# Identity products in TensorE's waits, two more units of cache kept in SBUF, and the first keys of the second layer in three pieces

## The chip, the cores and the metric

One core of one Trainium2 chip. The metric is the device time of the launch in microseconds, the median of several runs; lower is better.

## The reference

Two layers, each of which is an attention over a cached key and value store for one new token, and then a gated feed-forward block; both layers use the same weights and the same cache. Everything is 32-bit float.

```python
B, Sq, D = 2, 1, 512;  Hq, Hkv, Sk, Dh = 32, 8, 32768, 128;  Df = 1792
def _A_ref(x, k_cache, v_cache, wq, wo):
    q = (x @ wq)                       # per head, 4 query heads share one key head
    scores = einsum("bhqd,bhkd->bhqk", q, k) * (Dh ** -0.5)
    o = einsum("bhqk,bhkd->bhqd", softmax(scores), v)
    return o @ wo
def _B_ref(x, w_gate, w_up, w_down):
    return einsum("bsf,fd->bsd", gelu(x @ w_gate) * (x @ w_up), w_down)
x = A_x
x = x + _A_ref(_layernorm(x), ...);  x = x + _B_ref(_layernorm(x), ...)
x = x + _A_ref(_layernorm(x), ...);  x = x + _B_ref(_layernorm(x), ...)
```

The cache is the bulk: for each of 2 x 8 pairs of a sequence and a key head, 32768 keys and as many values of 128 numbers, 16 MB each.

## The kernel before

**Memory and units.** SBUF holds one large tile `M` of 110 units; a unit is 512 columns on 128 partitions, 256 KB. Units 0 to 95 are three slots of 32 (`SLOT_A`, `SLOT_B`, `SLOT_C`), each of which takes half of the keys or half of the values of one pair. Units 96 to 107 serve for weights; `PL` gives four places of 4 units there. `U_P0`, `U_P1`, `U_PT` (106 to 109) hold intermediate results when no weights stand there.

**The queue.** All loads are planned in one list in the order of their use, and SP issues them in this order. `free()` marks a unit as no longer needed; `pump()` then issues the loads at the head of the list whose places are free. An issue waits, on SP, for the instructions that read its place last, and for the landing of the load eight before it; all that is behind it in the list waits too.

**Attention.** `order1` gives the 16 pairs for the first layer; the second layer takes them in the opposite order, so that the last pair's cache can stay. For each pair, `scores` multiplies 32 key units per half (TensorE, `score_unit`, one unit is one product of 512 columns on one of four 32-row groups of the output bank), `peak` takes maxima, `softmax` exponentiates on ScalarE and transposes back, `values` multiplies 32 value units per half, and `combine` scales (ScalarE), transposes (TensorE) and reduces (VectorE). `project` adds the output projection into the bank `W`.

**Feed-forward.** `center` copies `W` (ScalarE), transposes it (TensorE) and makes the centred input (VectorE); `deviation` makes the norm's scale. `products(0)` and `products(1)` multiply 16 and 12 gate and up units, `gelu` is on ScalarE and VectorE, `hidden` transposes its result, and `down` multiplies 14 units. `restart` puts the residual back into `W`.

**The seam between the layers.** The last pair's values (64 units), the first 28 units of the second half of its keys (28 of `KC1`) and the last 5 units of the first half (in PSUM banks, `NPS`) are kept: 97 units. The other units of its keys are loaded again: 4 of the second half (`k1`) and 27 of the first half (`k0`, in pieces of 16 and 11, at units 64 to 90). In between the gate, up, down and query weights go through a ring of 16 units, in the order of `RING`: places 104, 92, 96 and 100, of 4 units each. The query products of the second layer alternate with scores on the kept keys. The keys of the second pair follow in pieces of 8, 8 and 16 at units 64 to 95, so that each needs the scores on the first pair's keys that stood there.

**The end.** The last layer's gate, up and down weights have slots of their own and no ring; they are loaded right behind the last values, and the last `down` is followed by one copy and the store.

PSUM banks in the order listings below: bank_79 is `A`, bank_80 is `W`, bank_81 is `X`, bank_74 and bank_75 take the scores.

Of the kernel before, what the change touches and what calls it, by code (L numbers as in the profile page):

```python
# [16 lines left out]
P = 128  # L17
# [18 lines left out]
PL = [96, 100, 104, 92]  # L36
# [10 lines left out]
KC1 = 28  # L47
NARROW = [6, 1]
NH = 2
NG = P // 16  # L50
WO_ORDER = {1: (2, 3, 0, 1)}
# [24 lines left out]
def block_kernel(ctx: ExitStack, tc: tile.TileContext, x, consts, kt, vt, wq, wo, wn, gu, wd, out):  # L76
# [90 lines left out]
    def ring_stream(name, l, src, total, at):  # L167
        cuts, places, n = [], [], 0
        while n < total:
            cuts.append(min(4, total - n))  # L170
            places.append(PL[RING[at % 4]])
            n += 4
            at += 1
        stream(name, l, src, total, cuts, places)
# [30 lines left out]
    for l in range(2):  # L205
        if l == 0:
            stream("wq", 0, wq, 32, (32,), (SLOT_C,))
            ring = [SLOT_A, SLOT_B, SLOT_C]
            todo = sequence(orders[0], 0)
            roles = [ring[(len(todo) - 4 + i) % 3] for i in range(3)]  # L210
        else:
            last0, last1, lastv = roles
            ring = [lastv, last0, last1]
            g, b = orders[1][0]
            assert last1 == SLOT_C
            add(("wq7",), cols(wq, 28, 4), ZONE + 2, 4)
            stream("wq", 1, wq, 28, (4, 2, 2, 4, 4, 4, 2, 2, 4), [ZONE + i for i in (6, 10, -4, -2, 2, 6, 10, -4, -2)])
            add(("k1",), cols(kt[b, g, 1], KC1, CH - KC1), ZONE + 2, CH - KC1)
            stream("k0", 1, kt[b, g, 0], KFREE, (16, 11), [last1, last1 + 16])
            g, b = orders[1][1]  # L220
            chunk("k", 1, g, b, 0, last1, (8, 8, 16))
            chunk("k", 1, g, b, 1, lastv)
            chunk("v", 1, g, b, 0, last0)
            add_wo(1, g)
            chunk("v", 1, g, b, 1, last1)
            todo = sequence(orders[1][2:], 1)
# [11 lines left out]
        if l == 0:  # L238
            ring_stream("gu", 0, gu, 28, 0)
            ring_stream("wd", 0, wd, 14, 7)  # L240
        else:
            stream("gu", 1, gu, 28, (8, 8, 4, 4, 4), [ring[(len(todo) - 3) % 3] + i for i in (0, 8, 16, 20, 24)])
            stream("wd", 1, wd, 14, (4, 4, 4, 1, 1), [ring[(len(todo) - 2) % 3] + i for i in (0, 4, 8, 12, 13)])
# [34 lines left out]
    def center():  # L278
        ws = mem(U_PT + 1)
        nc.scalar.activation(ws, W, AF.Copy, accum_out=rs)  # L280
        for c in range(KC):
            nc.tensor.transpose(X[:, c * P:(c + 1) * P], ws[:, c * P:(c + 1) * P], ident)
# [75 lines left out]
    def values(l, g, b, acc, wheres, keep, back):  # L358
        for h in range(2):
            where = wheres[h]  # L360
            for i in range(CH):
                key, u = where[i]
                if key:
# [4 lines left out]
                                 mem(u), start=(h == 0 and i < 4), stop=(h == 1 and i >= CH - 4))  # L368
                if not keep and i % back == back - 1:
# [3 lines left out]
    def combine(acc, oT, g, b):  # L373
        md = mem(U_PT)
        nc.scalar.activation(md, acc, AF.Copy, scale=linvc)  # L375
        for c in range(4):
# [29 lines left out]
    def feedforward(l):  # L406
# [8 lines left out]
        def products(v):  # L415
            s, nt = (0, 4) if v == 0 else (16, 3)
            for k in range(KC):
                for t in range(nt):
# [4 lines left out]
                    if cut[key] == s:  # L423
                        for q in range(28):
                            if where[q][0] == key:
                                free(where[q][1])
# [34 lines left out]
        def down(lo, hi):  # L461
            for n in range(lo, hi):
# [9 lines left out]
                free(un)  # L472

# [7 lines left out]
        hidden(1)  # L481
        down(8, FD)
# [10 lines left out]
    center()  # L493
# [15 lines left out]
    for n, (g, b) in enumerate(order1):  # L509
# [20 lines left out]
        values(0, g, b, A, [pieces[("v", 0, g, b, h)] for h in range(2)], (g, b) == last, CH)  # L530
        combine(A, oT, g, b)
# [17 lines left out]
    todo, s = deque(range(KC1)), 0  # L549
# [8 lines left out]
    for m in range(7):  # L558
# [10 lines left out]
        for j in range(min(early[m], len(todo))):  # L569
            i = todo.popleft()  # L570
            score_unit(S1, w, i, k1[i][1], i < 4, False)
# [4 lines left out]
    store(27, True)  # L576
    store(28, False)
# [7 lines left out]
    for i in range(KC1, CH):  # L585
        score_unit(S1, w, i, u + i - KC1, False, True)
    free(u, CH - KC1)
    peak(S1, 1)
# [18 lines left out]
    for n, (g, b) in enumerate(orders[1]):  # L607
# [7 lines left out]
        values(1, g, b, A, [pieces[("v", 1, g, b, h)] for h in range(2)], False, CH)  # L615
        combine(A, oT, g, b)
# [42 lines left out]
```

## Time and profile before

| | |
|---|---|
| runs | 2572.09, 2572.43, 2576.22 us |
| median | 2572.43 us |
| profiled execution, its own time | 2574.56 us |
| its span, first to last instruction | 2572.4 us |
| read from HBM | 1103.98 MB, 429 GB/s over the span |
| TensorE busy | 1354.3 us (53%) |
| mean granted TensorE clock | 0.741 |
| last values land, TensorE starts on them: first layer | 1285.50 us |
| the same, second layer | 2542.14 us |

A row of a timeline reads: start, length in us, engine, line, operation, output<-inputs, shape, number of instructions, and in brackets the idle time of the engine before it with what ended it. A 32-bit product stands in the trace as two records, a transpose as one. DMA issues stand with the engine that issues them (SPq), and a listing of issues ends with the time from issue to landing.

### The profile page before, as it was taken

To read this page: it belongs to the slowest core of one execution; us is meant where nothing else is said; L and a number is where in the kernel's file an instruction comes from. 1 tells how busy PE (TensorE), PEld (TensorE's weight loads), DVE (VectorE), ACT (ScalarE), POOL (GpSimd) and SP (SyncE) were. 2 spreads that over 40 slices of the span, in tenths; PEclk is the share of its full clock that TensorE was granted. 3 is DMA by queue.
4 is the path that set the end of the run, shared out by engine and by line. 5 is a ranking of instruction groups with operands and counts; after the bars stand their busy time and mean duration, and the time that the engine had idled before them with its cause. 6 is when DMAs were issued, how large, how long until landed. Compare 5 with 4: busy or idle time off the path is not lost.

```text
span 2572.4 us, 20214 instructions
## 1 busy us (share of the span) xinstructions
PE 1354.3 (53%) x9444; PEld 388.4 (15%) x9444; DVE 139.1 (5%) x459; ACT 83.4 (3%) x191; POOL 3.8 (0%) x12
## 2 busy tenths in 40 slices
PE   3545554445544555564576455454545544554556
PEld 1111111111111111111122111111111111111112
DVE  0000000000000000000011000000000000000001
ACT  0000000000000000000010000000000000000000
POOL 0000000000000000000000000000000000000000
PEclk9777777776777776777778777777777776777668
DMA  9999999999999999999999999999999999999998
GB/s 425 433 429 438 431 433 432 435 431 434 434 428 437 433 431 436 430 433 432 423 408 421 436 436 434 433 435 429 438 429 434 433 430 437 433 432 433 432 434 363
DMA packets 26187, 1105.34 MB, mean 430 GB/s; under 512 B 3032, under 2 KB 3288, under 8 KB 4312
## 3 DMA queue, kind: packets, MB, share of 16 engines
q1 hardware_dynamic: 25816, 1103.97, 99.5%
q8 instruction: 74, 1.21, 0.2%
q10 hardware_dynamic: 288, 0.09, 0.0%
q14 instruction: 9, 0.07, 0.0%
HBM read 1103.98 MB, written 0.07 MB: 429 GB/s over the span
## 4 chain that ended last, share of the span: by engine, by line
DMA 68%; PE 23%; another core or an unknown queue 8%; issue 0%; ACT 0%; DVE 0%; ACTq 0%; DVEq 0%; SPq 0%
DMA M<-in_vt 38%; DMA M<-in_kt 26%; PE bank L366 10%; PE bank L321 10%; DMA cst<-in_consts 2%; DMA M<-in_wd 1%; DMA M<-in_wq 1%; PE bank L297 1%; PE bank L421 0%; PE bank L388 0%; PE bank L377 0%; ACT M L375 0%; PE bank L402 0%; PE bank L349 0%
## 5 line engine op out<-in xcount | busy, mean ns | idle before, releaser
L321 PE MATMUL bank<-M,qw 128*32 128x512 f32 x4096 | 587.3, 736 | 534.7 <-DMA M<-in_kt 534.0
L366 PE MATMUL bank<-M 128*16 128x512 f32 x4096 | 578.3, 727 | 511.3 <-DMA M<-in_vt 511.3
L321 PEld LDWEIGHTS bank<-M,qw 128*32 128x32 f32 x4096 | 143.9, 132 | 966.7 <-DMA M<-in_kt 572.3
L366 PEld LDWEIGHTS bank<-M 128*16 128x16 f32 x4096 | 136.3, 112 | 926.5 <-issue 912.2
L324 DVE TENSOR_REDUCE sm<-bank 128x1 f32<-128x512 f32 x64 | 44.2, 691 | 1111.6 <-PE bank L321 1111.6
L346 ACT ACTIVATE M<-bank,sm 128x512 f32<-128x512 f32 x64 | 43.4, 682 | 1216.7 <-DVE sm L341 1216.7
L349 PE MATMUL bank<-cst,M 128*128 128x128 f32 x256 | 51.8, 353 | 42.2 <-ACT M L346 42.0
L380 DVE TENSOR_REDUCE oT<-bank 128x4 f32<-128x64 f32 x32 | 7.2, 224 | 1118.7 <-PE bank L377 1118.7
L375 ACT ACTIVATE M<-bank,sm 128x512 f32<-128x512 f32 x32 | 22.0, 687 | 1137.5 <-PE bank L366 1137.5
L350 DVE COPY M<-bank 128x512 f32<-128x512 f32 x64 | 43.9, 692 | 61.5 <-PE bank L349 61.5
L349 PEld LDWEIGHTS bank<-cst,M 128*128 128x128 f32 x256 | 37.8, 179 | 52.3 <-ACT M L346 52.3
L377 PE MATMUL bank<-cst,M 128*128 128x128 f32 x128 | 21.5, 291 | 25.8 <-ACT M L375 25.8
L340 PE MATMUL bank<-cst,sm 128*128 128x128 f32 x32 | 10.3, 323 | 35.1 <-DVE sm L339 35.1
L275 PE MATMUL bank<-cst,xin 128*2 128x128 f32 x32 | 5.0, 307 | 42.7 <-DMA cst<-in_consts 42.7
L421 PE MATMUL bank<-M,xw 128*32 128x512 f32 x112 | 21.0, 664 | 6.4 <-DMA M<-in_gu 4.3
L354 PEld LDWEIGHTS bank<-cst,sm 128*128 128x128 f32 x128 | 23.6, 258 | 0.0
L377 PEld LDWEIGHTS bank<-cst,M 128*128 128x128 f32 x128 | 13.7, 143 | 55.3 <-ACT M L375 55.3
L354 PE MATMUL bank<-cst,sm 128*128 128x4 f32 x128 | 21.4, 273 | 0.0
L297 PE MATMUL bank<-M,xw 128*32 128x512 f32 x128 | 19.7, 716 | 2.7 <-DMA M<-in_wq 1.9
L388 PE MATMUL bank<-M,oT 128*2 128x512 f32 x120 | 17.5, 621 | 5.1 <-DVE oT L380 5.1
L340 PEld LDWEIGHTS bank<-cst,sm 128*128 128x128 f32 x32 | 4.3, 133 | 64.1 <-DVE sm L339 64.1
L346 ACT ACTIVATION_READ_ACCUMULATOR M<-bank,sm 128x1 f32 x64 | 12.5, 196 | 0.0
(73 smaller groups left out, 140.4 us busy)
## 6 DMA issues: line engine op xcount, KB each, us to landing
M<-in_wo SPq DMA_DIRECT2D x6, 2048.0 KB, 53.1
M<-in_vt SPq DMA_DIRECT2D x6, 2048.0 KB, 43.9
M<-in_gu SPq DMA_DIRECT2D x10, 1024.0 KB, 17.0
M<-in_kt SPq DMA_DIRECT2D x2, 4096.0 KB, 15.1
M<-in_wd SPq DMA_DIRECT2D x6, 1024.0 KB, 16.5
M<-in_wq SPq DMA_DIRECT2D x6, 1024.0 KB, 8.7
M<-in_vt SPq DMA_DIRECT2D x4, 1024.0 KB, 47.1
M<-in_kt SPq DMA_DIRECT2D x2, 2048.0 KB, 11.0
```

What stands on the lines that cost most here:

```text
L297: nc.tensor.matmul(Q[32 * k:32 * k + 32, :], xw[:, k, XO - 2 * g:XO - 2 * g + 32], mem(u), start=start, stop=stop)
L321: nc.tensor.matmul(S[32 * t:32 * t + 32, :], w[:, 28 - 4 * c:60 - 4 * c], mem(u), start=start, stop=stop)
L324: nc.vector.tensor_reduce(mx[:, h:h + 1], S, axis=AX.X, op=OP.max)
L346: nc.scalar.activation(p[h], S[h], AF.Exp, bias=bias, scale=SCALE, accum_out=ls[:, h:h + 1])
L349: nc.tensor.transpose(S[h][:, k * P:(k + 1) * P], p[h][:, k * P:(k + 1) * P], ident)
L350: nc.vector.tensor_copy(mem(U_PT + h), S[h])
L354: nc.tensor.matmul(X[:, P:P + REP], ls[:, h:h + 1].to_broadcast([P, P]), mask, start=(h == 0), stop=(h == 1))
L366: nc.tensor.matmul(acc[32 * t:32 * t + 16, :], mem(U_PT + h)[:, k * P + 32 * t + 16 * e:k * P + 32 * t + 16 * e + 16], mem(u), start=(h == ...
L375: nc.scalar.activation(md, acc, AF.Copy, scale=linvc)
L377: nc.tensor.transpose(X[:, c * P:(c + 1) * P], md[:, c * P:(c + 1) * P], ident)
L388: nc.tensor.matmul(W[32 * t:32 * t + NB, :], oT[:, t, :], mem(u), start=(t > 0 and first), stop=final)
L421: nc.tensor.matmul(G[v][32 * t:32 * t + 32, :], xw[:, k, XO:XO + 32], mem(un), start=(k == 0), stop=(k == KC - 1))
```

## The change

Four things are changed together.

- **Kept and reloaded keys.** `KC1` goes from 28 to 30: 30 units of the second key half are kept (99 units in all), and 2 are loaded again. The ring loses two units: its places are 104 (4), 94 (2), 96 (4) and 100 (4), 14 units, and the weights' pieces are cut to fit. The order of the early scores, and the copies of the five units from PSUM to SBUF, are fitted to the new places.
- **The first half of these keys** comes in pieces of 8, 8 and 11 units in the place of 16 and 11.
- **Identity products.** `fill(n)` issues n products of 32 columns of the identity with the identity three times over (384 columns); the result goes to the last 32 partitions of `X`, columns 128 and up, and is read by nothing. They stand in the last `values` of each layer (3 after unit 15, 1 after unit 23, 3 after unit 27 of the second half), in the `combine` behind it (2), in each `center` but the first (2), after each piece of gate and up weights but the first and the last (half its units), after the fourth unit of `down` (2), and behind the second `hidden` (2): 54 in all, 27 from the first layer's last values to the first query products of the second layer, 27 from the second layer's last values on.
- **The last down weights** come in pieces of 4, 4, 2, 2, 1, 1 in the place of 4, 4, 4, 1, 1.

```diff
-PL = [96, 100, 104, 92]
+PL = [96, 100, 104, 94]
+SIZE = [4, 4, 4, 2]
...
-KC1 = 28
+KC1 = 30
...
+GAPS = {15: 3, 23: 1, 27: 3}
...
         while n < total:
-            cuts.append(min(4, total - n))
-            places.append(PL[RING[at % 4]])
-            n += 4
+            i = RING[at % 4]
+            cuts.append(min(SIZE[i], total - n))
+            places.append(PL[i])
+            n += SIZE[i]
             at += 1
...
-            add(("wq7",), cols(wq, 28, 4), ZONE + 2, 4)
-            stream("wq", 1, wq, 28, (4, 2, 2, 4, 4, 4, 2, 2, 4), [ZONE + i for i in (6, 10, -4, -2, 2, 6, 10, -4, -2)])
-            add(("k1",), cols(kt[b, g, 1], KC1, CH - KC1), ZONE + 2, CH - KC1)
-            stream("k0", 1, kt[b, g, 0], KFREE, (16, 11), [last1, last1 + 16])
+            add(("wq7",), cols(wq, 28, 4), ZONE + 8, 4)
+            stream("wq", 1, wq, 28, (4, 4, 4, 2, 2, 4, 4, 4), [ZONE + i for i in (-2, 2, 6, 10, -2, 0, 4, 8)])
+            add(("k1",), cols(kt[b, g, 1], KC1, CH - KC1), ZONE - 2, CH - KC1)
+            stream("k0", 1, kt[b, g, 0], KFREE, (8, 8, 11), [last1, last1 + 8, last1 + 16])
...
-            stream("wd", 1, wd, 14, (4, 4, 4, 1, 1), [ring[(len(todo) - 2) % 3] + i for i in (0, 4, 8, 12, 13)])
+            stream("wd", 1, wd, 14, (4, 4, 2, 2, 1, 1), [ring[(len(todo) - 2) % 3] + i for i in (0, 4, 8, 10, 12, 13)])
...
+    spin = ident.unsqueeze(1).to_broadcast([P, 3, P])
+
+    def fill(n):
+        for _ in range(n):
+            nc.tensor.matmul(X[96:, P:].rearrange("p (c d) -> p c d", c=3), ident[:, :32], spin, start=True, stop=True)
+
-    def center():
+    def center(n=2):
         ws = mem(U_PT + 1)
         nc.scalar.activation(ws, W, AF.Copy, accum_out=rs)
+        fill(n)
...
+                if gaps and h == 1:
+                    fill(gaps.get(i, 0))
...
-    def combine(acc, oT, g, b):
+    def combine(acc, oT, g, b, n=0):
         md = mem(U_PT)
         nc.scalar.activation(md, acc, AF.Copy, scale=linvc)
+        fill(n)
...
                     if cut[key] == s:
-                        for q in range(28):
-                            if where[q][0] == key:
-                                free(where[q][1])
+                        units = [where[q][1] for q in range(28) if where[q][0] == key]
+                        for un in units:
+                            free(un)
+                        if s < 27 and not (v == 0 and k == 0):
+                            fill(len(units) // 2)
...
                 free(un)
+                if n == 3:
+                    fill(2)
...
         hidden(1)
+        fill(2)
         down(8, FD)
...
-    todo, s = deque(range(KC1)), 0
+    first = [*range(18), 28, 29, *range(18, 28)]
+    ends = {i % 4: i for i in [*first, 30, 31]}
+    todo, s = deque(first), 0
...
-    store(27, True)
-    store(28, False)
     store(29, True)
...
     free(u, CH - KC1)
+    store(27, True)
+    store(28, False)
     peak(S1, 1)
```

SP's issues behind the query weights at the seam, before (the shape is partitions x columns; 512 columns are a unit; `in_kt` are keys):

```order
L120 DMA M<-in_wq 128x1024 x2
L120 DMA M<-in_wq 128x2048
L120 DMA M<-in_kt 128x2048
L120 DMA M<-in_kt 128x8192
L120 DMA M<-in_kt 128x5632
L120 DMA M<-in_kt 128x4096 x2
L120 DMA M<-in_kt 128x8192
```

and in the change:

```order
L122 DMA M<-in_wq 128x2048 x3
L122 DMA M<-in_kt 128x1024
L122 DMA M<-in_kt 128x4096 x2
L122 DMA M<-in_kt 128x5632
L122 DMA M<-in_kt 128x4096 x2
L122 DMA M<-in_kt 128x8192
```

The reload of the second half has 2 units in the place of 4, and the 16 units of the first half are two issues of 8.

TensorE from the last layer's last 24 value units to the first gate and up products, before (L366 values, L377 and L282 transposes, L388 output projection, L421 gate and up):

```order
L366 MATMUL bank_79<-M 16x512 x64
L377 MATMUL bank_81<-cst,M 128x128 x4
L388 MATMUL bank_80<-M,oT_69 2x512 x4
L282 MATMUL bank_81<-cst,M 128x128 x4
L283 MATMUL bank_79<-cst,sm 128x2
L421 MATMUL bank_79<-M,xw 32x512 x4
```

and in the change, where L285 is `fill`:

```order
L376 MATMUL bank_79<-M 16x512 x48
L285 MATMUL bank_81<-cst 32x384 x3
L376 MATMUL bank_79<-M 16x512 x8
L285 MATMUL bank_81<-cst 32x384
L376 MATMUL bank_79<-M 16x512 x4
L285 MATMUL bank_81<-cst 32x384 x3
L376 MATMUL bank_79<-M 16x512 x4
L285 MATMUL bank_81<-cst 32x384 x2
L390 MATMUL bank_81<-cst,M 128x128 x4
L401 MATMUL bank_80<-M,oT_69 2x512 x4
L285 MATMUL bank_81<-cst 32x384 x2
L292 MATMUL bank_81<-cst,M 128x128 x4
```

Three groups of products stand between the pieces of the values, two ahead of the transposes of `combine`, and two ahead of those of `center`. The first layer's last pair has the same rows.

TensorE from the gate and up products of the last layer on, before (L272 `restart`, L450 `hidden`, L467 `down`):

```order
L421 MATMUL bank_79<-M,xw 32x512 x12
L421 MATMUL bank_81<-M,xw 32x512 x12
L272 MATMUL bank_80<-cst,xin 2x128 x4
L450 MATMUL bank_79<-cst,M 128x8 x2
L467 MATMUL bank_80<-M,hT 2x128 x32
L450 MATMUL bank_81<-cst,M 128x8 x2
L467 MATMUL bank_80<-M,hT 2x128 x24
```

and in the change, from the second piece of the gate and up weights on:

```order
L285 MATMUL bank_81<-cst 32x384 x4
L434 MATMUL bank_79<-M,xw 32x512 x8
L285 MATMUL bank_81<-cst 32x384 x4
L434 MATMUL bank_81<-M,xw 32x512 x4
L285 MATMUL bank_81<-cst 32x384 x2
L434 MATMUL bank_81<-M,xw 32x512 x4
L285 MATMUL bank_81<-cst 32x384 x2
L434 MATMUL bank_81<-M,xw 32x512 x4
```

```order
L482 MATMUL bank_80<-M,hT 2x128 x16
L285 MATMUL bank_81<-cst 32x384 x2
L482 MATMUL bank_80<-M,hT 2x128 x16
L465 MATMUL bank_81<-cst,M 128x8 x2
L285 MATMUL bank_81<-cst 32x384 x2
L482 MATMUL bank_80<-M,hT 2x128 x24
```

Four products stand behind each of the two pieces of 8 units, two behind the pieces of 4, two between the fourth and the fifth unit of `down` (L482, four products to a unit), and two behind the second `hidden` (L465).

More of the change, by code (lines that the diff above doesn't have):

```diff
@@ L239, in block_kernel @@
             ring_stream("gu", 0, gu, 28, 0)
-            ring_stream("wd", 0, wd, 14, 7)
+            ring_stream("wd", 0, wd, 14, 8)
         else:
             stream("gu", 1, gu, 28, (8, 8, 4, 4, 4), [ring[(len(todo) - 3) % 3] + i for i in (0, 8, 16, 20, 24)])
-            stream("wd", 1, wd, 14, (4, 4, 4, 1, 1), [ring[(len(todo) - 2) % 3] + i for i in (0, 4, 8, 12, 13)])
+            stream("wd", 1, wd, 14, (4, 4, 2, 2, 1, 1), [ring[(len(todo) - 2) % 3] + i for i in (0, 4, 8, 10, 12, 13)])
     nc.scalar.dma_start(xin, x)
@@ L356, in softmax, with values @@
         nc.vector.tensor_tensor_reduce(junk, linv, mask, 1.0, 0.0, OP.mult, OP.add, linvc)
-    def values(l, g, b, acc, wheres, keep, back):
+    def values(l, g, b, acc, wheres, keep, back, gaps=None):
         for h in range(2):
@@ L492, in block_kernel @@
     restart(True)
-    center()
+    center(0)
     where = pieces[("wq", 0)]
@@ L529, in block_kernel @@
             softmax(S)
-        values(0, g, b, A, [pieces[("v", 0, g, b, h)] for h in range(2)], (g, b) == last, CH)
-        combine(A, oT, g, b)
+        end = (g, b) == last
+        values(0, g, b, A, [pieces[("v", 0, g, b, h)] for h in range(2)], end, CH, GAPS if end else None)
+        combine(A, oT, g, b, 2 * end)
         if b == 1:
@@ L570, in block_kernel @@
             i = todo.popleft()
-            score_unit(S1, w, i, k1[i][1], i < 4, False)
+            score_unit(S1, w, i, k1[i][1], i < 4, ends[i % 4] == i)
             free(k1[i][1])
@@ L585, in block_kernel @@
     for i in range(KC1, CH):
-        score_unit(S1, w, i, u + i - KC1, False, True)
+        score_unit(S1, w, i, u + i - KC1, False, ends[i % 4] == i)
     free(u, CH - KC1)
+    store(27, True)
+    store(28, False)
     peak(S1, 1)
@@ L614, in block_kernel @@
         softmax(S)
-        values(1, g, b, A, [pieces[("v", 1, g, b, h)] for h in range(2)], False, CH)
-        combine(A, oT, g, b)
+        end = n + 1 == len(order1)
+        values(1, g, b, A, [pieces[("v", 1, g, b, h)] for h in range(2)], False, CH, GAPS if end else None)
+        combine(A, oT, g, b, 2 * end)
         if b == 0:
```

## The prediction

> **What bounds the kernel now.** I read the page first, for the share of each engine. The first row is the span, the second the busy share of the 16 DMA engines in 40 slices, the third the chain that ended last, and the fourth the costliest group.
>
> ```profile
> span 2572.4 us, 20214 instructions
> DMA  9999999999999999999999999999999999999998
> DMA 68%; PE 23%; another core or an unknown queue 8%; issue 0%; ACT 0%; DVE 0%; ACTq 0%; DVEq 0%; SPq 0%
> L321 PE MATMUL bank<-M,qw 128*32 128x512 f32 x4096 | 587.3, 736 | 534.7 <-DMA M<-in_kt 534.0
> ```
>
> The DMA engines work from the first slice to the last; TensorE idles for half of the score line and nearly all of that idle ends with a landing. So time goes only by fewer bytes, by a DMA engine that runs out of work, or in what follows the last landing. The second view is a table of stretches around the two places that the change touches: the seam between the layers and the end. Columns: stretch, length, five engines' busy time, PE clock, DMA share, GB/s.
>
> ```profile
> 1277.00:1287.00 10.00, 5.40 (x48) 0.78 (x40) 0.00 (x0) 0.38 (x1) 0.00 (x0) 1.00 1.00 417
> 1287.00:1297.00 10.00, 8.16 (x36) 3.17 (x40) 1.25 (x10) 0.99 (x3) 0.69 (x1) 0.50 0.82 315
> 1351.90:1354.00 2.10, 1.33 (x12) 0.12 (x4) 0.00 (x0) 0.00 (x0) 0.00 (x0) 1.00 0.89 290
> 2537.00:2567.00 30.00, 19.98 (x192) 6.83 (x196) 5.83 (x24) 4.09 (x9) 0.99 (x2) 1.00 0.90 377
> ```
>
> Two dips of the DMA share at the seam: 1287 to 1297 us, with the clock at 0.50, and 1352 to 1354 us; the third row is the end. Whether a dip costs anything is told by landings, since all later work waits for those. Third view: single issues of SP, each by its start and then with its time to landing.
>
> ```profile
> 1290.74 0.33 SPq L120 DMA_DIRECT2D M<-in_gu  x1
> M<-in_gu SPq DMA_DIRECT2D x1, 1024.0 KB, 7.0
> 1295.18 0.33 SPq L120 DMA_DIRECT2D M<-in_gu  x1
> M<-in_gu SPq DMA_DIRECT2D x1, 1024.0 KB, 5.1
> 1337.70 0.33 SPq L120 DMA_DIRECT2D M<-in_kt  x1
> M<-in_kt SPq DMA_DIRECT2D x1, 2816.0 KB, 16.3
> 1351.09 0.33 SPq L120 DMA_DIRECT2D M<-in_kt  x1
> M<-in_kt SPq DMA_DIRECT2D x1, 2048.0 KB, 9.7
> 1353.31 0.33 SPq L120 DMA_DIRECT2D M<-in_kt  x1
> M<-in_kt SPq DMA_DIRECT2D x1, 2048.0 KB, 12.4
> ```
>
> The gu pieces of 4 units (a unit is 256 KB) land at 1290.74 + 7.0 = 1297.7 and 1295.18 + 5.1 = 1300.3: 2.5 us apart, 0.62 a unit. That is the ordinary pace, so the first dip delays no landing: only engines that were ahead pause. The second does. The piece of 11 units lands at 1354.0, the next 8 units at 1351.09 + 9.7 = 1360.8, the 8 after them at 1353.31 + 12.4 = 1365.7. Eight units take 4.9 us there, but the first took 6.8: **1.9 us lost**, because that piece was issued only 2.9 us before the landing ahead of it. What held the issue stands in the timeline of TensorE:
>
> ```profile
> 1347.39 5.84 PE L321 MATMUL bank<-M,qw 128*32 128x512 f32 x32 [6.45 <-DMA M<-in_kt]
> 1354.08 3.68 PE L321 MATMUL bank<-M,qw 128*32 128x512 f32 x32 [0.85 <-DMA M<-in_kt]
> ```
>
> The first key piece holds 16 units, TensorE idles 6.45 us until all have landed, and the next chunk's first 8 units go to the places of its first 8.
>
> **The change part by part.** *Bytes.* Two units fewer of the first keys come a second time: 2 x 256 KB, at 0.62 us a unit **-1.2 us**. The DMA engines have no idle time to absorb them in, so I give it no range.
>
> *Kept K in 8, 8, 11.* The first 8 units land 8 x 0.61 = 4.9 us before the 16 did, so at about 1342.4 less the 1.2 above. Their scores, 3.4 us at half clock (twice the 0.86 us below, doubled), free the places at about 1344.6; the 8-unit issue then comes some 6 us earlier than 1351.09, and the landing ahead of it, 1354.0 - 1.2, is 8 us off. At the gu pieces an issue 1297.7 - 1295.18 = 2.5 us ahead cost nothing. Late next would be the 8 units behind it: their places free after the second 8, landed at about 1346.1, at 1349.5, again 8 us ahead. The gain lies between 0 (the one delayed piece was a chance matter) and the row's 1.9; I take **-1.9**, since the row's dip and the late issue coincide.
>
> *The ring of 14.* Units in flight behind the last values shrink from 16 to 14, 8.7 us of transfer. What refills it first is the place of the first gu piece, freed by the first four products. The chain until then:
>
> ```profile
> 1280.53 1.91 PE L366 MATMUL bank<-M 128*16 128x512 f32 x16 [2.14 <-DMA M<-in_vt]
> 1285.50 1.05 PE L366 MATMUL bank<-M 128*16 128x512 f32 x8 [1.43 <-DMA M<-in_vt]
> 1287.36 1.12 PE L377 MATMUL bank<-cst,M 128*128 128x128 f32 x4 [0.81 <-ACT M L375]
> 1291.48 1.12 PE L282 MATMUL bank<-cst,M 128*128 128x128 f32 x4 [0.81 <-ACT M L280]
> 1293.18 1.93 PE L421 MATMUL bank<-M,xw 128*32 128x512 f32 x8 [0.36 <-DVE xw L285]
> ```
>
> Before, it takes 1295.1 - 1285.5 = 9.6 us, at half clock from 1287. In the changed order 18 units land ahead of the piece that waits here, the last at 1285.5 + 18 x 0.62 = 1296.7; with the lead of 2.5 us that sufficed, the issue must come by 1294.2. So the smaller ring needs the chain in 8.7 us, 0.9 less than it takes, which the identity products would have to give.
>
> *The identity products (fills).* One fill has a moving operand of 384 columns and holds one of four 32-column groups. Four units on the four groups take 8 records in 1.91 - 1.05 = 0.86 us at full clock, though one record takes 736 ns in the mean: the groups run side by side, and 512 columns hold a group 0.86 us. It so holds its group 0.86 x 384/512 = **0.64 us** (estimate), 1.28 at half clock. There are 54 of them: 27 at each place, or 17 us. At the seam, three fills (1.9 us) behind unit 15 stand in a wait of 2.14, one in the short wait behind unit 23, three in a wait of 1.43, where they end 0.3 us after the landing. The two in combine take 1.28 against a wait of 0.81, likewise the two in center: about +0.3, +0.3 and +0.3 to the chain. Does the clock hold? Three stretches of 3.41 us, the step in which it moves:
>
> ```profile
> 1283.62:1287.03 3.41, 1.50 (x15) 0.13 (x8) 0.00 (x0) 0.41 (x1) 0.00 (x0) 1.00 1.01 416
> 1317.75:1321.17 3.42, 2.06 (x17) 0.80 (x14) 0.16 (x1) 0.58 (x1) 0.69 (x1) 1.00 1.02 412
> 1307.51:1310.92 3.41, 1.95 (x19) 0.36 (x18) 2.23 (x7) 1.07 (x3) 0.31 (x1) 1.00 1.02 428
> ```
>
> After the first two it fell, after the third not, so PE time alone does not decide, but 1.50 us plus five fills is nearly a whole step. I take it to hold. The same chain at full clock stands at the end of the kernel, below: from landing to the start of the first products 2548.06 - 2542.14 = 5.92 us, plus 1.06 for them, plus the 0.9 above, 7.9 us. The issue comes at 1293.4, 0.8 us in time: the ring costs **0**, bounded by 0 and, at half clock, the third rival's price. That a faster TensorE at the seam gains nothing else follows from the landings there being on pace.
>
> The Trainium skill ("TensorE: Matmul & The Clock Gate", "Why this matters for your kernels") asks for no gaps above some 3 us between bursts. By that rule the clock would have held without fills, since none of the gaps above behind 1280 is longer than 2.14 us; the 0.50 of 1287 to 1297 us contradicts it here. By the rule the sum is the same and the third rival has no chance; I go by the row.
>
> *The fills at the end.* There the clock was 1.00 without them (2537 to 2567 us), so they buy little and may cost.
>
> ```profile
> 2546.82 0.66 PE L282 MATMUL bank<-cst,M 128*128 128x128 f32 x4 [0.81 <-ACT M L280]
> 2548.06 1.06 PE L421 MATMUL bank<-M,xw 128*32 128x512 f32 x8 [0.46 <-DVE xw L285]
> 2549.36 1.06 PE L421 MATMUL bank<-M,xw 128*32 128x512 f32 x8
> 2551.95 1.92 PE L421 MATMUL bank<-M,xw 128*32 128x512 f32 x16 [1.52 <-DMA M<-in_gu]
> 2554.50 1.88 PE L421 MATMUL bank<-M,xw 128*32 128x512 f32 x8 [0.62 <-DMA M<-in_gu]
> 2542.14 1.05 PE L366 MATMUL bank<-M 128*16 128x512 f32 x8 [1.43 <-DMA M<-in_vt]
> 2551.97 0.33 SPq L120 DMA_DIRECT2D M<-in_wd  x1
> M<-in_wd SPq DMA_DIRECT2D x1, 256.0 KB, 16.1
> 2564.32 1.06 PE L467 MATMUL bank<-M,hT 128*2 128x128 f32 x32 [0.95 <-DMA M<-in_wd]
> 2566.91 2.67 PE L467 MATMUL bank<-M,hT 128*2 128x128 f32 x48 [0.99 <-DMA M<-in_wd]
> 2569.62 0.29 DVE L485 COPY M<-bank 128x128 f32<-128x128 f32 x1 [3.49 <-PE bank L467]
> L421 PEld LDWEIGHTS bank<-M,xw 128*32 128x32 f32 x112 | 4.0, 115 | 19.1 <-DMA M<-in_gu 8.7 <-issue 7.3 <-DVE M L439 2.1
> ```
>
> Combine and center bring +0.9 as at the seam. The gu pieces of 8 units now draw four fills each, 2.56 us. Behind the first, TensorE is free from 2549.36 + 0.86 = 2550.22 to 2551.95, 1.73 us: +0.8. Behind the second it is free 0.8 us, and the next units use the other three groups and can start with the last record of the fills, 0.32 us before their end: 2.24 - 0.8 = +1.4. The pieces that follow come in before at the DMA's pace; now they have landed already, and work off some 1.2 us of this. So the products end 0.9 + 0.8 + 1.4 - 1.2 = 1.9 us late. Then come two fills between the fourth and fifth unit of the down projection, and two behind the second hidden transpose, on whose copy the units behind them wait anyhow: 4 x 0.64 = +2.6. The waits of 0.95 and 0.99 ahead of those units take up 1.9 of it, and full clock for the last 48 records (2.67 before; 1.06 x 48/32 = 1.6) another 1.1. I get 1.9 + 2.6 - 1.9 - 1.1 = **+1.5 us**, the last record's end at 2571.1 in the place of 2569.6. The last weights land at 2551.97 + 16.1 = 2568.1, so this end is TensorE's. Bounds: below, -1.0, if the fills cost nothing and the end follows 0.5 us behind that landing (2568.6); above, +3.7, if each of some ten fills on the path also pays for two loads of 32 columns of weights, 0.115 us each in the last row.
>
> Sum: -1.2 - 1.9 + 0 + 1.5 = **-1.6 us**. The profiled execution had 2574.56 us around its span of 2572.4, so 2573.0 for such a one; the median of the runs is 2572.43, so **2570.8**.
>
> **The rivals.** *First: the fills hide at the end as well*, since units in other groups run beside them; the landings then end the kernel: -1.2 - 1.9 - 1.0 = -4.1, 2568.3. For it: the groups do overlap (736 ns against eight records in 0.86 us). Against it: most units come in fours, and the fourth needs the fills' group. The Trainium skill ("TensorE: Matmul & The Clock Gate", "Packing small matmuls") lets matmuls of distinct column groups run at once, starts 4 ns apart; it speaks for this rival as far as groups differ. *Second: the late piece was chance.* Then 1.9 is not won: -1.2 + 1.5 = +0.3, 2572.7. For it: the issue at 1351.09 was still 2.9 us ahead, more than the 2.5 that sufficed at the gu pieces. Against: the dip to 290 GB/s. *Third, slower: the ring of 14 dries up.* If the clock falls at 1287 all the same, each fill costs 1.28: two in combine and two in center add 2.56 - 0.81 = 1.75 each to the 9.6 us, the issue comes at 1285.5 + 13.1 = 1298.6 in the place of 1294.2, and 4.4 us of landings are lost: -1.6 + 4.4 = +2.8, 2575.2. It decides from a chain of 8.7 us on. The fills not doing what they are for ends here too.
>
> **How the numbers follow.** Chances: forecast 0.48, first rival 0.22, second 0.16, third 0.14. The lowest case is 2568.3 and the highest 2575.2; with 0.8 us below and 0.3 above for the spread of runs, the range is 2567.5 to 2575.5, and leaves out combinations such as the third rival with dear fills at the end (2575.2 + 3.7 - 1.5 = 2577.4). About 0.2%, 5.1 us, is what a measurement of this kernel tells from no change. No case reaches it alone: same 0.86; faster 0.08 (the first rival with more won at the seam than I see); slower 0.06 (the third with the dear end).
>
> **What would show it.** HBM read falls by 0.5 MB. The granted clock of 1287 to 1297 us rises to 1.00; at 0.50 the third rival is on. The issue behind the first 8 kept units comes near 1345 us, and the pieces at 1354 to 1361 land 4.9 us apart; a gap above 6 is the second rival. The last record before the closing copy ends about 3.0 us after the last weights land; 0.5 would be the first rival. A median outside 2567.5 to 2575.5 says that a transfer far from both places moved, which nothing above foresees.

## The result, and the profile after

| | before | changed |
|---|---|---|
| median | 2573.07 us (22 runs, 2571.40 to 2576.31) | 2577.57 us (22 runs, 2574.53 to 2579.34) |
| span of the profiled execution | 2572.4 us | 2575.6 us |
| last values of the first layer land | 1285.45 us | 1285.17 us |
| second pair's second key half (32 units) lands, after those values | 109.4 us | 112.7 us |
| from there to the landing of the second layer's last values | 1147.2 us | 1147.6 us |
| from there to the end | 30.3 us | 30.1 us |

The ratio is 1.0015, 95% interval [1.0009, 1.0021]: the changed kernel is slower, by some 4.5 us in the medians and 3.2 us in the two profiled executions. The medians here and below leave out two runs at a much lower clock, one of 2637.28 us and one of 6135.87 us (of the kernels e1 and e9 further down). The forecast was 2570.8 us, its range 2567.5 to 2575.5. The middle and the end take what they took before; the 3.3 us arise within 113 us behind the first layer's last values. That landing of the second pair's key half is called **the seam's end** below, since from it on the kernels run alike.

A landing is the last of sixteen reports that the trace has for each load, and the sixteen can lie far apart: those of the seam's end span 2.61 us before and 1.14 us in the changed kernel. So the mean of the sixteen, the **mean report**, is given beside it. By mean reports the seam's end is 110.7 us behind the first layer's last values before and 114.9 in the changed kernel, 4.2 us later and nearer to the 4.5 of the medians.

First the page of the changed kernel: its span, the DMA engines' busy share and the rate in 40 slices, and the bytes.

```profile
span 2575.6 us, 20428 instructions
DMA  9999999999999999999999999999999999999998
GB/s 424 435 428 435 432 431 435 431 436 428 435 434 427 438 433 430 434 430 433 420 395 401 436 436 434 433 432 429 436 432 431 436 432 430 438 430 432 434 432 370
HBM read 1103.45 MB, written 0.07 MB: 428 GB/s over the span
```

The bytes fell by 0.53 MB, as forecast. The busy share shows nothing: a 9 is 90% or more. The rate shows it: the 21st and 22nd slice (1288 to 1417 us) move 395 and 401 GB/s. The same rows before have 408 and 421:

```profile
GB/s 425 433 429 438 431 433 432 435 431 434 434 428 437 433 431 436 430 433 432 423 408 421 436 436 434 433 435 429 438 429 434 433 430 437 433 432 433 432 434 363
```

Then the table of stretches, in which the columns are as in the prediction (PE clock, DMA share and GB/s stand last). Before:

```profile
1297.00:1310.00 13.00, 9.46 (x64) 2.65 (x56) 4.16 (x13) 2.72 (x6) 0.31 (x1) 0.99 1.01 421
1320.00:1330.00 10.00, 10.00 (x64) 3.68 (x60) 0.34 (x2) 0.00 (x0) 0.00 (x0) 0.66 1.02 418
1350.00:1360.00 10.00, 7.24 (x57) 1.79 (x49) 1.21 (x4) 0.46 (x1) 0.00 (x0) 0.91 0.94 376
1360.00:1370.00 10.00, 9.62 (x72) 3.37 (x76) 1.62 (x5) 0.99 (x4) 0.00 (x0) 0.83 1.06 453
1370.00:1380.00 10.00, 9.19 (x88) 2.69 (x84) 0.22 (x1) 0.69 (x1) 0.00 (x0) 1.00 1.04 436
1290.00:1400.00 110.00, 81.06 (x573) 25.76 (x573) 12.90 (x48) 9.06 (x20) 1.69 (x3) 0.83 1.01 420
```

And after:

```profile
1287.00:1297.00 10.00, 9.22 (x60) 3.65 (x59) 1.26 (x10) 0.98 (x3) 0.70 (x1) 1.00 0.89 342
1297.00:1310.00 13.00, 10.98 (x74) 3.93 (x70) 3.98 (x13) 2.72 (x6) 0.31 (x1) 1.00 1.00 400
1320.00:1330.00 10.00, 8.22 (x66) 2.68 (x64) 0.49 (x3) 0.59 (x1) 0.69 (x1) 1.00 0.94 339
1320.50:1322.00 1.50, 1.38 (x12) 0.46 (x11) 0.16 (x1) 0.45 (x1) 0.69 (x1) 1.00 0.74 213
1350.00:1360.00 10.00, 5.21 (x36) 1.21 (x32) 0.00 (x0) 0.00 (x0) 0.00 (x0) 0.76 0.98 419
1360.00:1370.00 10.00, 7.68 (x45) 3.56 (x41) 2.86 (x9) 1.45 (x4) 0.00 (x0) 0.73 0.94 377
1370.00:1380.00 10.00, 10.00 (x100) 2.53 (x96) 0.00 (x0) 0.00 (x0) 0.00 (x0) 1.00 0.91 362
1372.00:1376.00 4.00, 4.00 (x40) 0.96 (x36) 0.00 (x0) 0.00 (x0) 0.00 (x0) 1.00 0.40 168
1290.00:1400.00 110.00, 83.32 (x589) 27.80 (x591) 12.84 (x48) 8.93 (x20) 1.69 (x3) 0.92 0.98 399
```

These rows count a packet, with all its bytes and its time, in the stretch in which it starts. A packet of 64 KB takes 2.4 us here, so short neighbouring stretches exchange bytes; shares above 1.00 are a sign of it. Spread over the time that each packet takes, the same traces give, in GB/s:

| stretch, us | 1287 to 1297 | 1297 to 1310 | 1320 to 1330 | 1350 to 1360 | 1360 to 1370 | 1370 to 1380 | 1380 to 1390 |
|---|---|---|---|---|---|---|---|
| before | 317 | 420 | 419 | 387 | 428 | 418 | 429 |
| changed | 339 | 399 | 340 | 429 | 358 | 308 | 433 |

No 10 us of either trace move more than 435. The 453 and 436 of the rows before are bytes that the row of 1350 to 1360 lacks, and not a faster stretch.

Two places lose. **In the ring** the rate is 399 in the place of 420 GB/s from 1297 to 1310 us, and 340 in the place of 419 from 1320 to 1330, all at a clock of 1.00: TensorE is fast there, and the DMA engines run dry all the same. **At the key pieces** it is 358 and 308 from 1360 to 1380, where before had 428 and 418; the DMA engines are at a share of 0.63 in the 4 us from 1372 on (0.40 in the row, by the packets that start there). The stretch from 1350 to 1360 gained, 429 against 387, as the shorter pieces were to bring.

What happens at the key pieces stands in the timeline of TensorE after, with the issues of the two loads behind:

```profile
1349.52 1.92 PE L331 MATMUL bank<-M,qw 128*32 128x512 f32 x16 [0.76 <-DMA M<-in_kt]
1356.23 6.49 PE L331 MATMUL bank<-M,qw 128*32 128x512 f32 x32 [4.79 <-DMA M<-in_kt]
1362.86 0.33 SPq L122 DMA_DIRECT2D M<-in_kt  x1
1375.45 0.33 SPq L122 DMA_DIRECT2D M<-in_kt  x1
M<-in_kt SPq DMA_DIRECT2D x1, 22.5
```

With the second 8 units done early, TensorE now idles 4.79 us ahead of the last piece, where it idled 0.85. The granted clock falls to 0.5 from 1355.17 to 1362.00 us, and the same 32 records take 6.49 in the place of 3.68 us. They free the places of the 16-unit load (issued at 1362.86, before at 1357.87) and lead to the softmax and the first values, whose places the 32-unit load waits for (1375.45, before 1370.79). It lands 22.5 us after its issue, at 1397.9.

### The profile page after: what moved, and what is told of

The parts are those of the page before. It is cut to its first block, busy times and chain, and to the rows that moved or that the text cites. A ratio compares the mean times of both kernels' runs of the same rounds, so it can differ in the third digit from the quotient of the medians.

```text
span 2575.6 us, 20428 instructions
## 1 busy us (share of the span) xinstructions
PE 1367.7 (53%) x9552; PEld 396.4 (15%) x9552; DVE 139.0 (5%) x459; ACT 83.5 (3%) x191; POOL 3.8 (0%) x12
## 4 chain that ended last, share of the span: by engine, by line
DMA 69%; PE 23%; another core or an unknown queue 8%; issue 0%; ACT 0%; DVE 0%; ACTq 0%; DVEq 0%
DMA M<-in_vt 42%; DMA M<-in_kt 24%; PE bank L376 11%; PE bank L331 9%; DMA cst<-in_consts 2%; PE bank L285 1%; DMA M<-in_wq 1%; PE bank L307 1%; PE bank L434 0%; DMA M<-in_wd 0%; DMA M<-in_gu 0%; PE bank L401 0%; PE bank L390 0%; PE bank L482 0%
## 5 line engine op out<-in xcount | busy, mean ns | idle before, releaser
L360 DVE COPY M<-bank 128x512 f32<-128x512 f32 x64 | 43.9, 691 | 61.8 <-PE bank L359 61.4
L285 PE MATMUL bank<-cst 128*32 128x384 f32 x108 | 38.6, 487 | 0.5 <-DVE hT L466 0.5
L285 PEld LDWEIGHTS bank<-cst 128*32 128x32 f32 x108 | 11.4, 110 | 24.5 <-issue 21.8
## 6 DMA issues: line engine op xcount, KB each, us to landing
M<-in_wd SPq DMA_DIRECT2D x5, 1024.0 KB, 24.8
```

Of the source, the lines that this page charges most:

```text
L285: nc.tensor.matmul(X[96:, P:].rearrange("p (c d) -> p c d", c=3), ident[:, :32], spin, start=True, stop=True)
L360: nc.vector.tensor_copy(mem(U_PT + h), S[h])
```

## The experiments

Each kernel was timed beside the kernel before. "Seam's end" is the landing defined above, and "mean report" the same by the mean of the sixteen reports, both from one profiled execution of each; "rate" is that of the row of 1290 to 1400 us. e4, e5, e6, e9 and e12, like e1, keep the finer last down weights too.

| kernel | ring | first keys | identity products | median, us | ratio to before | seam's end, us | mean report, us | rate, GB/s |
|---|---|---|---|---|---|---|---|---|
| before | 16 | 16, 11 | none | 2573.1 to 2573.5 | | 109.4 | 110.7 | 420 |
| changed | 14 | 8, 8, 11 | all | 2577.57 | 1.0015 [1.0009, 1.0021] | 112.7 | 114.9 | 399 |
| e4 | 16 | 16, 11 | all | 2572.42 | 0.9998 [0.9989, 1.0006] | 107.6 | 110.2 | 422 |
| e1 | 14 | 16, 11 | all | 2575.32 | 1.0005 [0.9996, 1.0015] | 111.5 | 112.1 | 408 |
| e2 | 16 | 8, 8, 11 | none | 2575.82 | 1.0006 [0.9998, 1.0015] | 113.0 | 114.9 | 402 |
| e3 | 14 | 8, 8, 11 | none | 2578.34 | 1.0017 [1.0008, 1.0025] | 117.0 | 118.7 | 380 |
| e5 | 14 | 8, 8, 11 | all, and in the key waits | 2576.26 | 1.0009 [1.0000, 1.0018] | 110.3 | 112.1 | 409 |
| e6 | 16 | 8, 8, 11 | all, and in the key waits | 2573.42 | 1.0000 [0.9992, 1.0009] | 107.7 | 109.3 | 422 |
| e7 | 16 | 16, 11 | seam only | 2572.24 | 0.9997 [0.9988, 1.0006] | 109.0 | 110.4 | 421 |
| e8 | 16 | 8, 8, 11 | seam, and in the key waits | 2572.73 | 0.9997 [0.9988, 1.0006] | 109.0 | 110.9 | 420 |
| e9 | 14, 28 kept | 16, 11 | all | 2576.56 | 1.0014 [1.0005, 1.0023] | 112.5 | 114.5 | 404 |
| e10 | 16 | 16, 11, half in 16 + 16 | none | 2573.43 | 1.0000 [0.9991, 1.0009] | 110.7 | 110.7 | 418 |
| e11 | 16 | as e8, half in 16 + 16 | as e8 | 2571.87 | 0.9995 [0.9987, 1.0004] | 108.6 | 109.6 | 422 |
| e12 | 14 | as changed, half in 16 + 16 | all | 2575.23 | 1.0007 [0.9998, 1.0015] | 109.4 | 111.4 | 415 |

The intervals of e1 to e12 are some 2.3 us to either side, so a difference of 2 us between two of these kernels is a trend and no proof by itself; what carries the reading is that pairs with the same difference agree.

**The parts apart (e1 to e4).** e1 undoes the 8, 8, 11 alone; e4 keeps the identity products (and the finer last weights) alone; e2 adds the 8, 8, 11 alone to the kernel before; e3 takes the identity products, and the finer last weights, out of the changed kernel.

```diff
# e1, and e4 (which also has the ring of 16 and 28 kept units again)
-            stream("k0", 1, kt[b, g, 0], KFREE, (8, 8, 11), [last1, last1 + 8, last1 + 16])
+            stream("k0", 1, kt[b, g, 0], KFREE, (16, 11), [last1, last1 + 16])
# e2, against before
-            stream("k0", 1, kt[b, g, 0], KFREE, (16, 11), [last1, last1 + 16])
+            stream("k0", 1, kt[b, g, 0], KFREE, (8, 8, 11), [last1, last1 + 8, last1 + 16])
# e3
-        for _ in range(n):
+        for _ in range(0):
```

> The changed kernel with the first half of the last pair's keys in 16 and 11 units again (identity products and the ring of 14 stay). Measure: the time from the landing of the first layer's last values to the landing of the second pair's 32-unit key half, 109.4 us before and 112.7 in the changed kernel. Cold-scores theory (the pieces of 8, 8, 11 let TensorE idle 4.8 us ahead of the last one, its clock falls, the 32 records behind it take 6.5 us in the place of 3.7, and the next two key issues come 5 us late): the 32 records are back at 3.7 us, the 2.8 us lost at the 32-unit half return, the 1.9 us at the first 8-unit piece are lost again: about 111.8, median about 2576.6. Ring theory (the 14 units are what costs): the pieces were a gain, so this is slower: 114.6, about 2579.5.

> The kernel before with only the pieces of 8, 8 and 11. Cold-scores theory: 1.9 us won at the first 8-unit piece, 2.8 to 3.5 lost behind it: 110.3 to 111.0 us from values to the 32-unit half, median about 2574 to 2575. Ring theory: only the gain is left, 107.5 us, about 2571.2. In both, the clock of the values step stays as before (0.5 from 1287 to 1297 us).

> The changed kernel without any identity product (and the last down weights in their former pieces); ring of 14 and pieces of 8, 8, 11 stay. Cold-scores and ring theories: the loss stays or grows, since the ring of 14 meets the half clock: 112.7 us or more from values to the 32-unit half, median 2577.6 to 2581. If the identity products themselves cost (they hold TensorE ahead of the first products and the query weights), it falls to about 109, median about 2574.

> The kernel before with only the identity products (and the last down weights in the changed pieces); ring of 16, keys in 16 and 11. Cold-scores and ring theories: no loss, 109.4 us or a little less, the end as in the changed kernel (30.1 us from the last values to the end against 30.3): median 2572 to 2573. If the identity products themselves cost: 1.5 to 3 us slower, 2574.5 to 2576.

One chain of steps holds all three parts: before 2573.2, with the identity products (e4) 2572.4, with the ring of 14 as well (e1) 2575.3, with the 8, 8, 11 as well (changed) 2577.6. So the identity products gave some -0.8 us (which e4's interval does not tell from nothing), the ring +2.9 with its fewer bytes, and the 8, 8, 11 +2.2; e2 agrees on the last with 2575.82, 2.6 us above before. e3 says that the identity products were not what cost: without them it is 2578.3. Of e2 one thing must be kept apart: its profile had already lost 1.9 us when the last first-key piece landed, with the clock at 0.53 from 1320 to 1330 us, ahead of all that the cut can have changed. From that piece to the seam's end it still takes 2.1 us more than before, by mean reports (42.43 and 40.35 us).

**The clock at the key pieces (e5 to e8).** If the idle time ahead of the last piece costs by the clock, identity products in the two waits should give it back. e5 puts 3 behind the first 8 key units and 6 behind the second; e6 is the same with the ring of 16 and 28 kept; e7 is the kernel before with the identity products of the seam alone, and e8 joins e7 with the 8, 8, 11 and those in the waits.

```diff
         score_unit(S0, w, i, u, i % 4 not in seen, left[i % 4] == i)
         seen.add(i % 4)
         free(u)
+        fill({7: 3, 15: 6}.get(i, 0))
```

> The changed kernel with two more groups of identity products, in the waits between the first pair's key pieces: 3 behind the first 8 units and 6 behind the second 8. Cold-scores theory: the clock holds at 1.00 until the softmax, the 32 records behind the last piece take 3.7 us in the place of 6.5, the issues of 16 and 32 units come 3 to 5 us earlier, and the time from the landing of the first layer's last values to that of the 32-unit key half falls from 112.7 to about 110, the median by 2.5 to about 2575. If the half clock there is not what makes them late, nothing changes: 112.7, about 2577.6.

> The same with the ring of 16 and 28 units kept. Ring of 14 as the larger cause (the identity products with the ring of 16 measured 107.6 us, with the ring of 14 111.5): the time from values to the 32-unit half is 106 to 107 us, and the median 2571 to 2572.5, the fills at the end costing 1 us. If the ring is not the cause: as the run before this one, about 110 us.

> The kernel before with identity products from the first layer's last values to the second layer's first query products alone, none at the end (last down weights in their former pieces too). If the fills gain 1.8 us at the seam and cost 1.3 at the end: 107.6 us from values to the 32-unit half, 29.2 to 30.3 us from the second layer's last values to the end, median 2570.5 to 2571.5. If the end's 31.6 us of the run with all fills was chance: the end stays near 30.3 to 31.6 and the median at 2572.4.

> The same with the keys in 8, 8 and 11 units and 3 and 6 identity products in the waits between them. With the clock held there, the pieces should at last gain: 105.9 us from values to the 32-unit half is what 173 units take at the pace of 0.617 us a unit in the seam and 0.608 in the large pieces; I expect 106 to 107 and a median of 2569.5 to 2571. If the pieces cost for another reason than the clock, 108 to 111 us and 2572 to 2575.

In e5 the timeline at that place reads:

```profile
1349.20 2.14 PE L331 MATMUL bank<-M,qw 128*32 128x512 f32 x16
1351.17 4.03 PE L285 MATMUL bank<-cst 128*32 128x384 f32 x12
1355.91 3.68 PE L331 MATMUL bank<-M,qw 128*32 128x512 f32 x32 [0.71 <-DMA M<-in_kt]
```

The last 32 records take 3.68 us again, the seam's end comes 2.4 us earlier than in the changed kernel and the median is 1.3 us lower. The stretch from the last first-key piece to the seam's end, by mean reports, tells it apart from the ring: it takes 42.4 to 43.9 us in the three kernels with 8, 8, 11 and nothing in the waits (changed, e2, e3), 39.5 to 40.8 in the three with products there (e5, e6, e8), and 40.3 to 41.4 in the six with 16, 11 (before, e1, e4, e7, e9, e10). So the fall of the clock was that part of the loss. What stays, 2.8 us between e5 and e6, is the ring, much as between e1 and e4 (2.9). With ring and clock both mended (e6) the 8, 8, 11 still wins nothing over the 16, 11 of e4: 2573.4 and 2572.4 us, seam's end 107.7 and 107.6.

**The ring, and what the 32-unit load waits for (e9 to e12).** The first eight suggested theory A: in every kernel, before too, the seam's end follows the issue of the 32-unit load by 22.0 to 24.8 us, so that issue alone sets it. Its rival B was that in the kernel before the DMA engines are busy up to that landing, and only bytes set it. e10 to e12 load that half in two loads of 16, of which the first can start when half of the value places are free. e9 takes the kept units back to 28 and leaves the ring of 14, to tell whether it is the ring or the reordered scores that cost.

```diff
# e10 (on before), e11 (on e8), e12 (on the changed kernel)
-            chunk("k", 1, g, b, 1, lastv)
+            chunk("k", 1, g, b, 1, lastv, (16, 16))
# e9 (on e1)
-KC1 = 30
+KC1 = 28
-    first = [*range(18), 28, 29, *range(18, 28)]
-    ends = {i % 4: i for i in [*first, 30, 31]}
+    first = [*range(28)]
+    ends = {i % 4: i for i in [*first, 28, 29, 30, 31]}
```

> The changed kernel with the first keys in 16 and 11 as before, and with 28 kept units in the place of 30, so that the ring of 14 and its pieces are all that is left of that part (4 units come again, 1.2 us more of transfer). Theory, the ring of 14 itself starves the DMA engines: as the ring of 14 with 30 kept (2575.5 us, pair-two key half landed 111.5 us after the last values), plus 1.2: about 2576.7 us and 112.7, with the DMA rate of 1320 to 1330 us again near 345 GB/s. Rival, the kept units or the reordered early scores cost the time: as the ring of 16 with 28 kept and all fills, 2572.4 us and 107.6.

> The kernel before with one edit: the second pair's second key half (32 units) is loaded in two loads of 16, so that the first is issued when the first 16 value places of the slot are free, some 3.4 us earlier. Theory A, the landing of that half is set by its issue in every kernel, the one before too (it lands 22.0 to 24.8 us after the issue in all): it lands 106 us after the last values in the place of 109.4, and the median falls 2 to 3.4 us below before. Theory B, in the kernel before the DMA engines are busy up to it (436 GB/s from 1370 to 1380 us), so only bytes set it: 109.4, and the median of before.

> Ring of 16 and 28 kept, identity products at the seam alone and in the waits for the key pieces, keys in 8, 8, 11 (2572.7 us, half landed at 109.0), and now with that half in two loads of 16. Theory A (issue-bound): 105.6 and about 2569.5 us, the fastest of all. Theory B (bytes): 109.0 less at most what its last profile showed as a dip behind 1370 us, so 2571.7 to 2572.7.

> The changed kernel with one edit: that key half in two loads of 16. Its DMA rate falls to 168 GB/s from 1372 to 1376 us, ahead of the issue at 1375.45, and is 492 in the 4 us after, so some 1.7 us of transfer are lost there net of what is caught up. Theory B: those 1.7 us come back, half landed at about 111.0, about 2575.9 us. Theory A: 3.4 us, 109.3, 2574.2. If a dip there is made good later anyhow: 112.7 and 2577.6, no change.

e9 came where the ring theory put it: 2576.56 us (2576.7 expected) and 112.5 us (112.7). Its rates, and that of e4 in the same stretch behind them, are those of the ring and not of the kept units:

```profile
1297.00:1310.00 13.00, 10.71 (x71) 3.53 (x69) 3.38 (x11) 2.30 (x5) 0.31 (x1) 1.00 1.00 399
1320.00:1330.00 10.00, 7.90 (x66) 2.77 (x64) 1.09 (x4) 1.07 (x2) 0.69 (x1) 1.00 0.99 357
```

```profile
1320.00:1330.00 10.00, 8.30 (x68) 2.63 (x71) 0.34 (x2) 0.00 (x0) 0.00 (x0) 1.00 1.02 420
```

e10 felled theory A. Its first 16 units were issued at 1367.20 us, 3.6 us earlier than the 32 before, and the seam's end did not come earlier (110.7 against 109.4 us; 110.7 in both by mean reports), nor did the median fall. The trace of before had told it: from 1370 to 1380 us the engines are at a share of 1.00, and none was dry there. In the changed kernel it was another matter, 168 GB/s in the row of 1372 to 1376, and there the same edit (e12) brings that row to

```profile
1372.00:1376.00 4.00, 4.00 (x44) 1.13 (x40) 0.00 (x0) 0.00 (x0) 0.00 (x0) 1.00 1.01 430
```

with the seam's end 3.3 us earlier (109.4) and a median 2.3 us lower, where B expected 1.7. That 1.7 took the rows at their word; spread over the packets' time the rate of 1370 to 1380 us rises from 308 to 430 GB/s, which is 2.8 us of transfer. Some of the 3.3 is the clock, which in this execution let the 16-unit load be issued at 1361.08 and not at 1362.86. e11 has the lowest median of all, 2571.87 us, but its interval of [0.9987, 1.0004] holds no change: none of the twelve beats the kernel before by more than can be measured.

## Why the prediction was wrong

**Bytes, -1.2: right.** HBM read fell by 0.53 MB, and e9 against e1, which differ by the two units (and the order of the early scores), gives 2576.56 - 2575.32 = 1.24 us. With intervals of 2.3 us, so close an agreement is luck.

**Kept K in 8, 8, 11, -1.9: wrong, it is about +2.2.** Two steps failed. The first is "I take -1.9, since the row's dip and the late issue coincide". The issue did come earlier, at 1348.80 (near 1345 was forecast, but the first 8 units landed late, at 1344.59, behind the slow ring), and the two pieces at 1356 to 1361 land 4.90 us apart, as forecast:

```profile
1342.13 0.33 SPq L122 DMA_DIRECT2D M<-in_kt  x1
M<-in_kt SPq DMA_DIRECT2D x1, 2816.0 KB, 14.1
1348.80 0.33 SPq L122 DMA_DIRECT2D M<-in_kt  x1
M<-in_kt SPq DMA_DIRECT2D x1, 2048.0 KB, 12.3
```

But the 1.9 us were not lost by the whole: a landing is the last of its sixteen reports. Of the 11-unit piece before, thirteen reports come from 1352.03 to 1352.45 us and the last at 1354.04; of the 8 units behind it thirteen from 1357.92 to 1358.16 and the last at 1360.79. The mean report comes 5.76 us after that of the piece ahead, where the ordinary pace is 4.90: 0.9 us were there to be won. e10 and e7 keep gaps of 6.7 and 6.5 us between the landings at that place and are not slower, and with clock and ring mended (e6) the even landings win nothing over e4 that the medians show. That was the second rival's point, with its +0.3. In e4 the 16, 11 shows landings 4.89 apart with the issue 2.95 us ahead, just as far as before, so the gap itself was partly chance. The second is "Late next would be the 8 units behind it". I followed the freed places for two 8-unit pieces and stopped. The next are the 16 units and the 32 behind them, which hang on the last piece of the scores; its landing does not move, TensorE now idles 4.79 us ahead of it, and that idle time halves the clock for just the chain that frees their places.

**The ring of 14, 0: wrong, it is about +4.1** (e9 against e4, with bytes equal: 2576.56 - 2572.42; with the two units fewer, e1, +2.9). The step that failed is the rule taken from the gu pieces, that an issue "1297.7 - 1295.18 = 2.5 us ahead cost nothing", from which I concluded that the chain had 8.7 us. The chain was as I worked it out: the first refill was issued at

```profile
1293.39 0.33 SPq L122 DMA_DIRECT2D M<-in_gu  x1
1316.82 0.33 SPq L122 DMA_DIRECT2D M<-in_wq  x1
M<-in_wq SPq DMA_DIRECT2D x1, 1024.0 KB, 6.5
1320.30 0.33 SPq L122 DMA_DIRECT2D M<-in_wq  x1
M<-in_wq SPq DMA_DIRECT2D x1, 1024.0 KB, 5.5
```

1293.39 - 1285.17 = 8.2 us after the landing (7.9 forecast, 8.7 allowed). The rate still fell to 400 GB/s behind it. The rows below it show the rule fail: the piece issued at 1316.82 lands at 1316.82 + 6.5 = 1323.3, the next issue is at 1320.30, 3.0 us ahead of that, and from 1320.5 to 1322 us the engines move 213 GB/s at a share of 0.74. In the trace's packets, 16 are under way at 1320.7 us, 5 at 1321.2 and 16 again at 1321.8. The sixteen reports tell why: fourteen of that piece's come from 1321.07 to 1321.57 us, about 1 us behind the next issue, and the last at 1323.36. A landing is the last report; the engines that had done their part already stood still. Landings that are evenly spaced only show that one engine had work. (The last report stays some 1.6 us behind the others from the piece issued at 1309.30 on; a 16 KB load of instructions, which takes 1.10 us, stands in the trace at 1311.54, but that it is the cause is not shown.) I had read the dip of 315 GB/s from 1287 to 1297 as free because the landings behind it were on pace, but the engines ahead are what later pieces live on. Kernels with the ring of 16 have leads of 4.6 to 8.6 us from 1311 to 1330 us and move 418 to 421 there (before, e4, e6, e7, e8, e11; the row of 1320 to 1330), but for the two whose clock had fallen, to a mean of 0.66 and 0.62 from 1310 to 1320: e10, with a lead of 3.9, moves 398, and e2, with leads of 3.0 and 3.1, 359. So late issues and a low rate go together with either ring; no kernel varied the lead alone.

**The identity products at the seam: right in what they do, and not worth much.** The granted clock was 1.00 from 1269.84 to 1344.93 us, so the third rival's condition did not come true; yet its time, 2575.2, was nearest, since the ring dries at full clock too. Its price of 4.4 us for the ring is near the 4.1 measured by luck, since it is that of a half clock. The price of the products themselves was right:

```profile
1278.03 2.10 PE L285 MATMUL bank<-cst 128*32 128x384 f32 x6
1282.00 0.81 PE L285 MATMUL bank<-cst 128*32 128x384 f32 x2
```

Two more of them (four records) take 2.10 - 0.81 = 1.29 us, 0.645 each, against the estimate of 0.64. What they save is less sure than one profile of before made it look: e10, whose TensorE instructions are those of before, had the clock at 1.00 from 1269.4 to 1300.1 us without any (and at 0.50 for the 3.4 us behind).

```profile
1287.00:1297.00 10.00, 5.98 (x44) 1.99 (x44) 1.26 (x10) 1.07 (x3) 0.70 (x1) 1.00 0.92 362
```

So before's 0.50 in that stretch was one outcome of a clock that moves in steps of 3.41 us, which lie differently in each execution: it fell at 1287.03 us before and at 1300.09 in e10. With the ring of 14 the products are worth more: at the last first-key piece the mean report is 71.5 us behind the first layer's last values in the changed kernel and 74.8 in e3, which has none; the medians differ by 0.8 us, since the products cost some 0.9 at the end, as told below.

**The end, +1.5: right in kind, too large.** The last record ends at 2571.26 + 1.47 = 2572.73:

```profile
2566.79 1.48 PE L285 MATMUL bank<-cst 128*32 128x384 f32 x4
2569.95 0.51 PE L285 MATMUL bank<-cst 128*32 128x384 f32 x1 [0.27 <-DVE hT L466]
2571.26 1.47 PE L482 MATMUL bank<-M,hT 128*2 128x128 f32 x36
```

The next to last weights land at 2571.02, the last by the usual 0.64 later at 2571.7 (an estimate; its own record is missing), so the end is 1.1 us behind the landing, where I said 3.0 and the first rival 0.5. It varies: 1.7 in e1 and 2.7 in e4, against 0.4 to 0.5 in e2, e7 and e10, which have no products there. From the second layer's last values to the end, the six profiles without identity products there, other than before's own, take 29.2 to 29.3 us (e2, e3, e7, e8, e10, e11) and those with them 30.0 to 31.6 (changed, e1, e4, e5, e6, e9, e12): about +0.9, the finer last weights, which the same kernels have, included. Before's own 30.3 was an unlucky draw, its last 48 records at half clock (2.67 us against 1.61 in e10), which I took for the rule.

**The sum.** Forecast -1.2 - 1.9 + 0 + 1.5 = -1.6. By the runs: identity products at both places -0.8, ring with its bytes +2.9, 8, 8, 11 +2.2, together +4.4, against 4.5 measured; these are the links of one chain of medians, so that their sum is no check of its own. The profiled pair agrees on the place: the first layer's last values 0.3 us earlier, from them the last first-key piece +2.4 late, from there to the issue of the 32 units +2.5, from issue to landing -1.6 (engines had run dry ahead of it), +3.3 at the seam's end, and +0.1 behind it. By mean reports it is +1.2 at the last first-key piece and +3.0 from there to the seam's end.

**What stays open.** The two losses overlap: e12 and e5 each give back 1.3 to 2.3 us of the 4.5 by different means, and no kernel was run with both. Which of the ring's pieces would have to be smaller for 14 units to suffice was not tried. Why one of the sixteen reports trails stays open too.

## What to carry to other kernels

Do not judge a dip of the DMA rate by whether landings stay evenly spaced or come late: a landing is the last of sixteen reports, and the others may have waited (with evenly spaced landings in the ring) or lost less (0.9 us where the landing was 1.9 late). Count an issue's lead against the first reports of the load ahead; here a lead of 3.0 us on the last was about 1 us on the others, and leads of 4.6 us and more kept the rate. Read a rate over a few us only after a look at how long a packet takes. When a load is cut so that work starts earlier, follow the chain to the last piece: its landing has not moved, the idle time has only been pushed ahead of it, and there the clock pays for it. Before a single profile's clock is put into a sum, look for another execution of the same instructions.

## What the runs showed that was not expected

- An issue 3.0 us ahead of the landing in front of it left engines without work (213 GB/s for 1.5 us), while the pieces of 4 units there still land 2.5 to 2.7 us apart, until one of 2 units takes 2.20 us; two units of 256 KB less room cost about 4.1 us.
- The sixteen reports of the load at the seam's end lie 0.88 us apart in e4 and 4.15 in e10, which is as much as most of the kernels differ by there.
- The same instructions of TensorE had a granted clock of 0.50 in one execution (before) and 1.00 in another (e10) from 1287 to 1297 us.
